# A chunked mLSTM cell feeding a squared-ReLU FFN: chunks 4 and 5 moved to the quarter-array layout, and the first FFN2 placed ahead of the third FFN1

## The chip, the core and the metric

The kernel runs on one core of one Trainium2 chip. The metric is the device time of one execution in microseconds (us), lower is better. All counting below starts at 0: chunk `s` is tokens `128 s` to `128 s + 127`, group `g` is chunks `2g` and `2g + 1`. (The change's own words count from 1: its "chunks 5 and 6" are `s = 4, 5`, its "first" and "third group" are `g = 0, 2`.)

## What is computed

An mLSTM cell (4 batches, 8 heads, 768 tokens, head size 40) and then a feed-forward layer on its 3072 rows of 320 numbers. The reference, cut to its core:

```python
for t in range(S):
    m_new = np.maximum(f_gate[:, :, t] + m, i_gate[:, :, t])
    f_stab = np.exp(f_gate[:, :, t] + m - m_new)
    i_stab = np.exp(i_gate[:, :, t] - m_new)
    m = m_new
    C = f_stab[..] * C + i_stab[..] * np.einsum('bhd,bhe->bhde', vt, kt)
    n = f_stab[..] * n + i_stab[..] * kt
    h_tilde = np.einsum('bhde,bhe->bhd', C, qt)
    denom = np.maximum(np.abs(np.einsum('bhd,bhd->bh', n, qt)), 1.0)
    y[:, :, t] = sigmoid(o_gate[:, :, t]) * h_tilde / denom
x = y.transpose(0, 2, 1, 3).reshape(B * S, H * D)     # 3072 x 320
h = np.maximum(x @ w_in, 0.0)                         # w_in 320 x 2048
out = h * h @ w_out                                   # w_out 2048 x 320
```

## The kernel before

The recurrence is done in chunks of 128 tokens: 24 chunks, 6 per batch. For a chunk, `scores` (L554) multiplies keys by queries, `weigh` (L494) makes the decay weights with ScalarE from a broadcast gate row block `A` (loaded by `load_A`, L425, masked by `mask`, L465, on GpSimd), `weighted` (L587) multiplies both on VectorE, and an attend step multiplies the result by the values, adds what comes from the state `C` of the chunk before, and makes the next state. The rows then become `x`, and `x` is turned so that its columns lie on partitions (`xT`). FFN1 of a group of two chunks needs both `xT`; FFN2 needs the squared result `g2`.

There are two forms of this attend step.

- **Full array, chunks 0 to 5** (`X_SQ = 6`): `attend` (L609) uses 128x128 matmuls: `hi` (state times queries, L622), `dC` (new state, L634) and `hp` (weights times values, L645). VectorE joins and normalises them (`normalise`, L805), and `turn_rows` (L843) turns `x` with four matmuls and a ScalarE copy (L853).
- **Quarters, chunks 6 to 23**: `attend_begin` (L684) and `attend_end` (L743) use 64x64 quarters of the array (L708 state times queries, L727 weights times values, L738 new state). Between the two stands a one-element VectorE instruction, L700: it reads what the first half wrote, and the second half's L738 waits for it. The result is transposed by VectorE in 32x32 squares (L758) and then goes out to HBM and back: `store_num` (L772), `load_num` (L775), `normalise_turned` (L783) on VectorE, `store_rows` (L826), `load_rows` (L830), and a VectorE square transpose `turn_squares` (L838). All these transfers are issued by SyncE, whose queue is served in the order written: a transfer that waits holds up those behind it. This form needs the decayed queries `eA` (`decays`, L480, ScalarE; `scale_q`, L669, VectorE) and its state in another layout (`decay_C`, L674).

FFN1 of groups 0 and 1 is the plain product, four parts each (`ffn1`, L890). From group 2 on it is a seven-product scheme (`ffn1_open` L1058, `ffn1_rows` L1078, `ffn1_close` L1095) on sums of weights (`sums_of_win`, L1014: `WS[0]`, `WS[1]`, `WS[3]`, and F21 in place) and of x (`sums_of_x`, L1028). FFN2 of group 0 is plain (`ffn2`, L906); from group 1 on it is a seven-product scheme as well (`ffn2_fast`, L970), on sums of `w_out` (`sums_of_weights`, L935: T0, T1, T2, and in place) and of `g2` (`sums`, L948: S1, S2, A21 in place, S4). These sums are VectorE work.

The weights arrive as 64-bit words and are rounded to 32 bits in 18 pieces (10 of `w_in`, 8 of `w_out`): a SyncE `fetch` (L195), two ScalarE passes `words` (L212), three VectorE passes and one on GpSimd in `join` (L225).

The order on every engine is written out by hand (`manual_schedule`); there is no planner. The program has three stretches:

1. a start-up until chunk 2 (L1153 to L1223),
2. the loop `u = 0..7` (L1228 to L1293) with chunks 2 to 5: even `u` does scores and weights, odd `u` attends, and each `u` carries one part of FFN1 of group 0 or 1,
3. the loop over `parts` (L1317 to L1430): part `n` belongs to chunk `s = 6 + n // 4`, at step `at = n % 4`. Before the change the parts are FFN1 of group 2 (n = 0..3), FFN2 of group 0 (4..7), FFN2 of group 1 (8..11), FFN1 of group 3 (12..15), and so on.

## Time and profile before

| what | us |
|---|---|
| three runs: median, lowest, highest | 492.46, 490.75, 492.82 |
| the profiled execution, its own time | 491.22 |
| its span, first to last instruction | 489.4 |
| TensorE matmul (PE) busy in the span | 481.7 |
| TensorE weight loads (PEld) | 449.0 |
| VectorE (DVE) | 341.8 |
| ScalarE (ACT) | 240.4 |
| GpSimd (POOL) | 215.3 |
| granted TensorE clock | 0.999 |

The profile names an instruction by engine, source line, and the tiles that it writes and reads. A float32 matmul leaves two records and its weight load two, so a count of "x16" is eight matmuls. The chain of waits is the sequence of work that ended last, followed backwards from the end; the list of waits says which engine stood idle for which other. Times in a timeline are counted from the start of the span.

### The profile page before, as it was taken

The numbers are of one execution on the slowest core, as the hardware profiler recorded it, in microseconds if no ns is written. First come the engines' busy times: TensorE is split into PE (matmuls) and PEld (weight loads), VectorE is DVE, ScalarE is ACT, GpSimd is POOL, SyncE is SP. The second block draws the span as 40 slices with busy tenths as digits, with TensorE's granted clock in tenths as the row PEclk, the third lists the DMA queues.
The fourth block names the chain that finished last, engine by engine and source line by source line (L and its number), as shares of the span: only waits on it lengthen the run. The fifth ranks groups of instructions, "written<-read, shape, count | busy, mean of one in ns | idle before, by whom it ended". The sixth has DMA issues, their size and how long they took to land.

```text
span 489.4 us, 15237 instructions
## 1 busy us (share of the span) xinstructions
PE 481.7 (98%) x6169; PEld 449.0 (92%) x6169; DVE 341.8 (70%) x704; ACT 240.4 (49%) x531; POOL 215.3 (44%) x322
## 2 busy tenths in 40 slices
PE   9999999999999999999999999999999999999997
PEld 4886788897799999999999999999999999999996
DVE  7799767888946856957966956857856956635441
ACT  4676996764522650942742941742942640513300
POOL 6455533432679178078179078078174040020000
PEclk9999999999999999999999999999999999999999
DMA  9999997745878579758759778658665612200000
GB/s 185 227 243 227 304 230 183 151 84 140 171 130 199 120 138 225 134 107 212 135 99 219 140 117 208 134 109 213 123 106 129 149 51 82 55 28 2 3 27 29
DMA packets 191096, 68.08 MB, mean 139 GB/s; under 512 B 158833, under 2 KB 180241, under 8 KB 191025
## 3 DMA queue, kind: packets, MB, share of 16 engines
q1 hardware_dynamic: 185280, 57.50, 55.1%
q0 software_dynamic: 5600, 9.50, 8.1%
q8 instruction: 49, 0.80, 0.7%
q14 instruction: 23, 0.18, 0.1%
q10 hardware_dynamic: 144, 0.10, 0.1%
HBM read 54.77 MB, written 18.01 MB: 149 GB/s over the span
## 4 chain that ended last, share of the span: by engine, by line
PE 87%; ACT 5%; SPq 4%; DMA 3%; issue 1%; DVE 0%; ACTq 0%
PE h_ps L965 35%; PE h_ps L1041 26%; PE h_ps L1090 8%; PE h_ps L911 4%; PE h_ps L874 3%; PE numT L727 3%; PE numT L708 2%; DMA lent_t<-in_moe_w_in_dram 1%; PE numT L738 1%; SPq L210 1%; PE tp L575 1%; PE h_ps L575 1%; SPq L1151 1%; ACT g_c L511 1%; DMA raw<-in_moe_w_in_dram 1%; DMA og<-in_o_gate_dram 1%
## 5 line engine op out<-in xcount | busy, mean ns | idle before, releaser
L475 POOL TENSOR_SCALAR_AFFINE_SELECT A_bc<-A_bc 64x512 f32<-64x512 f32 x32 | 22.5, 704 | 80.4 <-ACT kq L492 57.9
L965 PE MATMUL h_ps<-T,S 128*128 128x160 f32 x352 | 51.7, 300 | 0.6 <-ACT g_c L1107 0.6
L1071 ACT COPY r_sb<-h_ps 128x512 f32<-128x512 f32 x18 | 10.5, 585 | 84.2 <-PE h_ps L1041 84.2
L965 PEld LDWEIGHTS h_ps<-T,S 128*128 128x128 f32 x352 | 48.9, 190 | 1.1 <-ACT g_c L1107 0.9
L965 PE MATMUL h_ps<-w_out,g 128*128 128x160 f32 x336 | 49.2, 303 | 0.0
L981 DVE TENSOR_TENSOR y_sb<-y_sb,h_ps 128x160 f32<-128x160 f32 x44 | 14.1, 320 | 47.7 <-PE h_ps L965 47.6
L965 PEld LDWEIGHTS h_ps<-w_out,g 128*128 128x128 f32 x336 | 46.1, 190 | 1.3 <-issue 0.5
L1041 PE MATMUL h_ps<-xT,w_in 128*128 128x128 f32 x320 | 42.8, 278 | 0.0
L1041 PE MATMUL h_ps<-lent_t,w_in 128*128 128x128 f32 x320 | 42.2, 275 | 0.0
L1041 PEld LDWEIGHTS h_ps<-xT,w_in 128*128 128x128 f32 x320 | 38.9, 192 | 1.4 <-issue 1.0
L1090 PE MATMUL h_ps<-xT,w_in 64*64 64x128 f32 x960 | 39.1, 272 | 0.0
L1041 PEld LDWEIGHTS h_ps<-lent_t,w_in 128*128 128x128 f32 x320 | 38.9, 192 | 0.2 <-issue 0.2
L1041 PE MATMUL h_ps<-lent_t 128*128 128x128 f32 x320 | 39.0, 275 | 0.0
L1041 PEld LDWEIGHTS h_ps<-lent_t 128*128 128x128 f32 x320 | 37.3, 192 | 0.0
L505 ACT ACTIVATE A_bc<-A_bc,b_R 128x64 f32<-128x64 f32 (+1 forms) x128 | 35.7, 361 | 1.8 <-POOL A_bc L475 1.4
L1090 PEld LDWEIGHTS h_ps<-xT,w_in 64*64 64x64 f32 x960 | 34.8, 133 | 1.3
L379 POOL DMA_DIRECT2D va<-in_v_dram x56 | 34.2, 619 | 1.8 <-DMA kq_rows<-in_q_dram 1.3
L758 DVE STREAM_TRANSPOSE tn<-numT 128x256 f32<-128x256 f32 x36 | 14.0, 428 | 28.5 <-PE numT L708 19.2
L874 PE MATMUL h_ps<-xT,w_in 128*128 128x256 f32 x128 | 30.1, 385 | 1.6 <-ACT xT L853 1.2
L874 PEld LDWEIGHTS h_ps<-xT,w_in 128*128 128x128 f32 x128 | 23.4, 190 | 6.1 <-POOL w_in L240 1.6
L1033 POOL TENSOR_TENSOR lent_t<-xT 128x128 f32<-128x128 f32 (+1 forms) x18 | 14.6, 833 | 32.7 <-DVE xT L840 32.7
L965 PE MATMUL h_ps<-w_out,g_c 128*128 128x160 f32 x192 | 28.0, 302 | 0.0
(218 smaller groups left out, 1150.0 us busy)
## 6 DMA issues: line engine op xcount, KB each, us to landing
A_bc<-a_slots SPq DMA_DIRECT2D x32, 256.0 KB, 4.4
num_rows<-tn SPq DMA_DIRECT2D x18, 256.0 KB, 2.3
kq<-num_rows SPq DMA_DIRECT2D x72, 64.0 KB, 2.1
raw<-in_moe_w_out_dram SPq DMA_DIRECT2D x7, 640.0 KB, 5.4
kqT<-kq_rows SPq DMA_DIRECT2D x34, 128.0 KB, 3.3
og<-in_o_gate_dram SPq DMA_DIRECT2D x24, 160.0 KB, 4.9
out_dram<-y_sb SPq DMA_DIRECT2D x24, 160.0 KB, 3.1
raw<-in_moe_w_in_dram SPq DMA_DIRECT2D x7, 512.0 KB, 6.9
```

The costliest lines, as they stand in the source:

```text
L379: eng.dma_start(dst[HALVES[n], PR * (1 - late_keys) : PR * (2 - late_keys)], src[HALVES[late_keys], PR * m : PR * (m + 1)],)
L475: nc.gpsimd.affine_select(part, part, compare_op=ALU.is_ge, fill=-1e30, base=0, pattern=[[0, PR], [0, 2], [1, DP]], channel_multiplier=-1,)
L505: nc.scalar.activation(A[0][:, x, to], A[0][:, x, to], AF.Exp, bias=b_R[:, b, c, own, x : x + 1],)
L727: nc.tensor.matmul(d["numT"][m][HALVES[e], i, t0:], lhsT=va_w[s % NKQ][keys, at * D1 : at * D1 + DP], rhs=rhs, start=(s % NB == 0 and i == ...
L758: nc.vector.transpose(to[:, 2 * m : 2 * m + 2], d["numT"][m].rearrange("p c t -> p (c t)"))
L874: nc.tensor.matmul(hs[i][:, n, :], lhsT=w_in[:, a, fb * P : (fb + 1) * P], rhs=xT[:, :, a, :], start=(n == 0 and a == 0), stop=False,)
L911: nc.tensor.matmul(o_ps, lhsT=st["g2", g][:, fb, j * P : (j + 1) * P], rhs=w_out[:, fb, :], start=(fb == 0), stop=(fb == NF - 1),)
L965: nc.tensor.matmul(to, lhsT=lhsT[:, p], rhs=rhs[:, p, :], start=(start and p == 0), stop=(p == NPAIR - 1), skip_group_check=True,)
L981: add = lambda to, a, b: nc.vector.tensor_tensor(to, a, b, op=ALU.add)
L1033: sub = lambda to, a, b: eng.tensor_tensor(to, a, b, op=ALU.subtract)
L1041: nc.tensor.matmul(to[:, n, :], lhsT=lhsT[:, 4 * q + n, :], rhs=rhs, start=(start and n == 0), stop=True, skip_group_check=True,)
L1090: nc.tensor.matmul(to[cols, n, :], lhsT=w_in2[rows, 4 * q + n, cols], rhs=rhs, start=(start and n == 0), stop=True, skip_group_check=True,)
```

## The change

- `X_SQ` goes from 6 to 4: chunks 4 and 5 use `attend_begin` and `attend_end`, and their `x` goes the HBM way. They keep their scores on full width, and their state stays in the older buffers (`C_flat`), of which chunk 4 reads the full layout and chunk 5 the quarter layout.
- In loop `u`: chunk 4's weights and decays are made at `u = 2` ahead of a rounding step, from the unmasked `A`, and masked afterwards (`mask_W`). `decays` and `scale_q` for chunks 4 and 5 are added, `turn_rows` of 4 and 5 is gone. `store_num`, `load_num`, `normalise_turned`, `store_rows`, `load_rows`, `turn_squares` of 4 and 5 are spread from `u = 5` to `n = 2`.
- FFN2 of group 0 becomes `n = 0..3` and FFN1 of group 2 `n = 4..7`. The four matmuls on the last two pieces of `w_out` rows come at the end of FFN2 (`F2`), with two PSUM banks open.
- FFN1 of group 2 no longer begins its first product ahead (`ffn1_begin` is gone).
- Loads of k and v of chunks 8 and 9 go from the SyncE queue (`u = 5, 7`) to the GpSimd queue (`n = 2, 3`); o gates of 8 to 11 come at `n = 3, 4`.
- `sums_of_win(3)` and `(2)` move to `n = 3`, `sums_of_weights` to `n = 3` (T0) and `n = 4` (T1, T2), `sums(1, ..)` S1 and S2 to `n = 6, 7`.
- Chunk 0's state is copied in its two diagonal halves in place of a product with a block mask.

The core of the diff:

```diff
-    KQ_SQ, X_SQ, ROT = 7, 6, 8
+    KQ_SQ, X_SQ, ROT = 7, 4, 8
...
-    def ffn2(g, j, part):
+    F2 = [(j, fb) for half in ((0, 8), (8, 14), (14, 16)) for j in range(GT) for fb in range(*half)]
+
+    def ffn2(step):
+        if step == 0:
+            st["o_ps"] = [ps_h.tile([P, W], F32, name="h_ps")[:, :DM] for _ in range(GT)]
+        for j, fb in F2[8 * step : 8 * step + 8]:
...
             if u == 2:
+                weigh(4, masked=True, vw=False)
+                decays(4)
                 rounding.words()
             weighted(s)
...
             if u == 2:
-                mask(s + 1)
                 rounding.join()
+                mask_W(4)
                 rounding.join()
-                weigh(s + 1, masked=True)
+                values(4)
                 rounding.words()
             else:
                 if u == 0:
                     relu_half()
-                weigh(s + 1, masked=(u == 0), vw=(u > 0))
+                weigh(s + 1, masked=(u != 6), vw=(u == 6))
+                if u == 4:
+                    mask_W(5)
                 square_half()
+                if u > 0:
+                    scale_q(s)
...
-            attend(s)
+            if s < X_SQ:
+                attend(s)
+            else:
+                attend_begin(s)
+                attend_end(s)
+                store_num(s)
...
-                rounding.join()
+                rounding.join(fetch=u < 7)
...
-            for r in {5: (8,), 7: (9,)}.get(u, ()):
-                load(r)
-            for r in {5: (7,), 7: (8,)}.get(u, ()):
-                pair_up(r)
+            if u == 5:
+                pair_up(7)
+            if u == 7:
+                load_A(7)
             if u > 4:
-                load_o(2 * s)
-                load_o(2 * s + 1)
+                load_num(s)
             transposes(s + 1, (True, True))
             rounding.words()
             ffn1(u // 4, u % 4)
             square_half()
+            if u == 5:
+                decays(5)
+            if u == 7:
+                normalise_turned(4)
+                store_rows(4)
+                rounding.fetch()
+                rounding.join()
...
+        if u == 6:
+            load_squares(7)
...
-    turn_rows(5)
-    load_squares(7)
...
-    parts = [(1, 2, i) for i in range(4)] + [(2, 0, i) for i in range(4)]
-    for g in range(1, NG):
+    parts = []
+    for g in range(NG):
         parts += [(2, g, i) for i in range(4)]
         if g + 2 < NG:
             parts += [(1, g + 2, i) for i in range(4)]
-    LAST = (17, 17, 17, 17, 18)
+    ROUNDED = (16, 18)
...
+        if n == 0:
+            turn_kq(7)
+            pair_up(8)
+            load_rows(4)
+            normalise_turned(5)
+            store_rows(5)
+            rounding.words()
...
+            if n == 1:
+                turn_squares(4)
+                load_rows(5)
             do(store_num, s)
-            do(load_num, s)
-            do(load_squares, s + 2)
+            if n == 1:
+                load_squares(8)
+                load_num(6)
+            else:
+                do(load_num, s)
+                do(load_squares, s + 2)
...
+        if n == 2:
+            weigh(7, masked=True)
+        if n == 3:
+            normalise_turned(6)
+            store_rows(6)
+            load_o(8)
+            load_o(9)
+            load_rows(6)
+            sums_of_win(3)
+            sums_of_win(2)
+        if n == 4:
+            sums_of_weights(1)
...
+            if n == 2:
+                turn_squares(5)
+                sums_of_x(2)
+            else:
+                do(normalise_turned, s)
+                do(store_rows, s)
...
+        if n in (2, 3):
+            load(6 + n)
+        if n == 4:
+            load_o(10)
+            load_o(11)
...
+        for x in {3: (0,), 4: (2,)}.get(n, ()):
+            sums_of_weights(x)
+        if n in (6, 7):
+            sums(1, slice(0, NPAIR), (n - 5,))
```

The new `mask_W` sets the weights of later tokens to zero in place of the `-1e30` that `mask` writes into `A`:

```python
def mask_W(s):
    nc.gpsimd.affine_select(
        st[s]["W"], st[s]["W"], compare_op=ALU.is_ge, fill=0.0, base=0, pattern=[[0, H], [1, P]],
        channel_multiplier=-1,
    )
```

## What the change should do: the prediction

> **What bounds the kernel now.** I read the page first: busy time by engine, then the shares of the chain.
>
> ```profile
> PE 481.7 (98%) x6169; PEld 449.0 (92%) x6169; DVE 341.8 (70%) x704; ACT 240.4 (49%) x531; POOL 215.3 (44%) x322
> ...
> PE 87%; ACT 5%; SPq 4%; DMA 3%; issue 1%; DVE 0%; ACTq 0%
> ```
>
> TensorE is the chain for 87% of the span. The chain in order of time says where: until 60.56 us it runs through ScalarE, transfers and their issue, from there to the end almost only through TensorE. So in the stretch that the change rewrites (59 to 130 us) a matmul removed is time gained, unless TensorE then waits. The list of TensorE's waits shows how few there are:
>
> ```profile
> PE h_ps L874 <- ACT xT L853: 1.2, 1, 1.2
> ...
> PE numT L738 <- DVE kq L700: 0.3, 1, 0.3
> ```
>
> The 1.2 us ends at 60.56, ahead of FFN1 at `u = 4`. The chain's rows price both forms of attend (start, us, what):
>
> ```profile
> 65.35 1.05 PE hi L622 x8
> 66.40 0.89 PE dC L634 x8
> 67.29 1.75 PE hp L645 x16
> ...
> 114.54 0.38 PE numT L708 x8
> 114.92 0.44 PE numT L727 x16
> 115.36 0.26 PE numT L738 x16
> 115.61 0.02 issue
> 115.64 0.17 DVE kq L700
> 115.80 0.04 issue
> 115.85 0.44 PE numT L738 x16
> 116.29 0.46 PE numT L727 x16
> 116.75 0.22 PE numT L708 x8
> 116.97 13.12 PE h_ps L911 x48
> ```
>
> Full array: 3.69 us for chunk 4. Quarters: 2.43 us for chunk 7, the stop for L700 included.
>
> VectorE is the next engine. In the stretches (PE, PEld, DVE, ACT, POOL busy) it is 82 and 89% busy while TensorE hardly waits:
>
> ```profile
> 91.06:110.04 18.98, 18.98 (x338) 18.39 (x337) 15.50 (x35) 12.60 (x26) 6.72 (x10) 1.00 0.58 103
> 110.04:130.09 20.05, 19.77 (x148) 13.86 (x152) 17.91 (x32) 10.82 (x26) 9.10 (x13) 1.00 0.62 145
> ```
>
> [...] a quarter matmul record L727 lasts 0.27 us, yet 16 take 0.44. [...] `num_rows<-tn` lands after a median 2.3 us, and SyncE waits for such a store 18 times, at most 4.0. [...]
>
> **The change part by part.** PE terms, from the chain:
>
> 1. Chunk 4's attend: 3.69 to 2.43, gain 1.26.
> 2. Chunk 5's attend: `hi` 1.05 and `hp` 1.75, 2.80 together; as quarters without a new state 0.38 + 0.44 + 0.46 + 0.22 and a stop of 0.25 to 0.3, 1.8. Gain 1.0.
> 3. Two `turn_rows`: 0.37 + 0.37 each, gain 1.47. Their ScalarE copies go too.
> 4. FFN1 of group 2: 6.50 + 1.77 + 6.45 + 1.91 = 16.63 before; the later groups' form, which it takes, is 3.57 + 1.77 + 9.13 + 1.91 = 16.38. Gain 0.25. FFN2 of group 0 keeps 32 matmuls (17.6). In chunk 7 FFN1's rows now stand between the halves and cover L700: gain 0.3.
> 5. The 1.2 us wait. ScalarE stood idle 4.27 us before the words at 48.93 (a raw piece was late), and ran without a pause to the copy that TensorE waited for. Chunk 4's weights (2.43 + 0.20) move from behind those words into that idle time, with `decays` (1.25): 3.9 us. `A` of chunk 4 was issued at 35.33, issued in 0.76, and landed 8.9 later: 45.0; 45.0 + 3.9 = 48.9, just in time. The copy then follows the relu of FFN1 part 3 (PE ends 57.5, relu 1.0, copy 0.5): about 59.1, and scores end at 59.3. Gain 1.1; if `A` is late, each us takes one from it, so 0 to 1.2.
>
> Sum of gains: 1.26 + 1.0 + 1.47 + 0.55 + 1.1 = 5.4.
>
> What is added beside TensorE. GpSimd: two `mask_W`, not in the trace; the nearest row is `mask` (1.09 to 1.28), which they replace, in gaps of 1.6 and more. Bound: 0 to 0.5; I take 0, it cannot gain. Chunk 5's `decays` (1.25) meets 1.55 of ScalarE idle. k and v of chunks 8, 9: 14 issues, 2 x 4.5 us on GpSimd's queue; behind them stands `mask` of chunk 8 at `n = 5`, some 8 us later, so 0. SyncE loses these and gains the round trips.
>
> The last pieces of `w_out`: after chunk 6's attend, VectorE does transposes, copies, a square transpose and the first join by 3.4 us, GpSimd adds 1.55: 5.0. First use is the fifth matmul of `n = 2`, at 4.4 + 2.2 = 6.6. Covered.
>
> **Where TensorE may now wait: L700 of chunk 7 (`n = 5`).** VectorE works in order, from chunk 6's attend to that L700 (steps from start to start in its timeline): transposes, copies 1.07; square transpose 0.46; two joins 3.8; `scale_q` 0.61; `weighted` 1.2; square transpose 0.46; `sums_of_x` 1.06 (8.7 so far); `normalise_turned` 1.84; two win sums 2.3; T0 to T2 4.26; U2 and U4 1.3. Together 18.4. TensorE reaches L738's second half after 3 x 4.4 (FFN2) + 3.57 + 1.1 + 1.77 = 19.6. So VectorE has 1.2 to spare, and `normalise_turned(6)` waits for a load that is behind five others on SyncE. From VectorE's transposes of chunk 5: store_num to next issue 2.0, load_num 2.3, store_rows(4) 0.4; its landing (109.66 to 113.24 in the trace) 3.6; load_rows(4) 1.9, store_rows(5) and landing 3.6, load_rows(5) 1.9, store_num(6) 0.35, load_squares(8) 2.5, load_num(6) 2.3, landing 2.1: 22.9. TensorE passes from there to the end of chunk 6's attend in 12.4, so the rows land at 10.5, when VectorE has been free since 8.7. It idles 1.8 and with small gaps 2.1; less the 1.2: a stall of 0.9.
>
> **And L700 of chunk 8 (`n = 9`).** In the same place two parts later in the trace before, VectorE starts FFN1's four adds at 167.33, does `turn_kq`, `weighted`, S3 and the y add, and L700 at 173.33; TensorE needs it at 173.95, 0.6 later. After the change S2 (1.2) and T3 (1.4) stand in this row too, and S1 ahead of it fills the 0.5 that VectorE waited at 202.55. 2.6 - 0.6 = 2.0 at most; as the adds can start some 0.5 before 167.33's place, 1.5. From `n = 10` on the order is as before.
>
> Net: 5.4 - 0.9 - 1.5 = 3.0 gained. Against the profiled execution's own 491.22 (span 489.4 and 1.8 around it): 488.2. That execution lies 1.2 below the median 492.46; the four known times average 491.8, so I forecast 491.8 - 3.0 = 488.8. About 0.5% (2.5 us) is what a measurement of this kernel can tell from no change.
>
> **Rivals.**
>
> - *No new stall.* If transfers land faster than their medians and VectorE's steps keep their covers: 491.8 - 5.4 = 486.4. For: DMA share falls to 0.58 in this stretch, and the SyncE queue loses 14 issues. Against: 18.4 of 19.6 leaves little.
> - *VectorE becomes the bound from `n = 1` to 9.* The sums of `w_in`, `w_out` and `g2`, which lay in FFN2 of group 0, now lie around FFN1's adds. If the two stalls double to 4.8: 491.8 - 0.6 = 491.2, between 490 and 493. For: 89% busy before. Against: the load is mostly the same work in another order.
> - *The SyncE round trips are late: slower.* One mechanism: the five stores and loads ahead of load_num(6) are each released by the landing before. At the longest waits in the trace before (4.0 for num_rows, 4.7 for x_rows, 6.2 for a load of xT) N of chunk 6 lands 8 to 9 us later, VectorE stands, and L700 of chunk 7 with it, us for us: 488.8 + 8 = 497. It decides for slower by over 0.5% from 5.5 us of lateness. For: DMA share was 0.9 at 60 to 91 us. Against: the later chunks' same transfers kept near the medians, and a one-hop delay is not five.
>
> **Numbers.** Forecast 0.46 (487.2 to 490.3), no stall 0.14, VectorE-bound 0.22, late round trips 0.18. Range 485.8 to 493.2: it holds the first three. Faster: nearly all of the forecast and no stall, 0.59. Same: the VectorE case and a rest, 0.24. Slower 0.17.
>
> **What would show it.** Right: L622 and L645 only for chunks 0 to 3; the FFN1 part of `u = 4` starts near 59.4; the `n = 8` scores near 127 in place of 130.09; new waits of PE for L700 or for U2, U4 near 111 and 131, 2 to 3 us in sum; a VectorE wait for `num_rows` of chunk 6. Wrong: a wait of TensorE over 3 us after 60 us, SyncE waiting over 4 us for `x_rows` near 90, or `n = 8` later than 130.

## The result: slower by 0.8%

| | us |
|---|---|
| before, six runs: median, lowest, highest | 492.32, 490.75, 492.9 |
| after, six runs: median, lowest, highest | 495.77, 494.76, 496.75 |
| after / before, 95% interval | 1.0077 [1.0055, 1.0099] |
| profiled execution after: own time, span | 496.75, 495.0 |

The forecast was 488.8, its range ended at 493.2. Medians here and below are over all executions of a kernel, while the ratios leave out those more than 1.5% above its quickest (three of e14's 22, one of e8's six). The two profiled executions lie 5.5 us apart, more than the medians (3.45), since the profiled one of before is a quick one and that of after the slowest of its six. All accounts below are between the two executions.

TensorE's own work did become less. The page of the changed kernel (busy us by engine; then shares of the chain):

```profile
PE 479.6 (97%) x6227; PEld 447.1 (90%) x6229; DVE 341.8 (69%) x719; ACT 242.7 (49%) x534; POOL 226.6 (46%) x335
...
PE 64%; DMA 10%; DVE 8%; POOL 5%; SPq 5%; ACT 4%; issue 3%; DVEq 0%; POOLq 0%; ACTq 0%
```

That is 2.1 us less of TensorE than before, but TensorE's share of the chain fell from 87 to 64%: in some places other engines and transfers now end last. TensorE's waits of after (us in total, times, longest):

```profile
PE h_ps L1089 <- DVE r_sb L1072: 3.2, 1, 3.2
PE numT L757 <- DVE kq L718: 1.8, 4, 0.8
...
PE h_ps L1056 <- issue: 0.8, 1, 0.8
PE h_ps L896 <- ACT xT L875: 0.8, 1, 0.8
PE numT L727 <- issue: 0.7, 1, 0.7
PE h_ps L980 <- DVE S L975: 0.7, 1, 0.7
```

Before, the list held 1.2, 0.3 and (at 353.00) 0.6 from 60 us on. (Lines of after: L718 is the stop, the one-element instruction between the halves, that was L700; L727, L746, L757 are the quarters that were L708, L727, L738. U2 and U4, L1072 and L1074, are VectorE's sums of FFN1's first products, and FFN1's rows, L1089, need U2. S1 and S2 are sums of `g2`, T0 to T3 sums of `w_out`; FFN2 at n = 8 needs S2.) The windows of after from the scores of chunk 6 on (n = 0 to 3, 4 to 7, 8 to 11; columns: length, busy PE, PEld, DVE, ACT, POOL, granted clock, DMA share, GB/s):

```profile
86.22:108.23 22.01, 21.16 (x179) 15.24 (x176) 17.59 (x37) 8.93 (x18) 12.85 (x17) 1.00 0.69 156
108.23:131.75 23.52, 20.36 (x321) 19.70 (x323) 19.79 (x40) 11.07 (x27) 12.78 (x19) 0.93 0.90 164
131.75:152.47 20.72, 19.27 (x265) 18.43 (x257) 15.82 (x28) 10.52 (x26) 14.72 (x23) 1.00 0.72 128
```

Where the time went, by start times of the same work in both:

| place | before | after | after is later by |
|---|---|---|---|
| scores of chunk 6 (n = 0) | 89.97 | 86.22 | -3.75 |
| n = 8 | 130.09 | 131.75 | 1.66 |
| last half of attend, chunk 8 (n = 9) | 137.0 | 140.6 | 3.6 |
| the same, chunk 10 | 173.8 | 179.0 | 5.2 |
| the same, chunk 22 | 393.8 | 399.8 | 6.0 |

So 3.75 us were gained and 5.41 lost again by n = 8: TensorE waited 4.0 us where it had waited 0.3 (22.01 - 21.16 and 23.52 - 20.36), and its busy time grew by 1.7. The granted clock of 0.93 in the 23.52 us accounts for the latter: 3.4 us at half clock (116.60 to 120.01) cost 1.7. In windows of 4 us one sees where: behind the 3.17 us wait.

```profile
113.00:117.00 4.00, 0.83 (x18) 0.63 (x20) 3.86 (x4) 0.00 (x0) 3.91 (x5) 0.95 1.42 164
117.00:121.00 4.00, 4.00 (x95) 3.83 (x88) 1.72 (x4) 0.00 (x0) 0.00 (x0) 0.62 0.67 167
121.00:125.00 4.00, 4.00 (x37) 4.00 (x38) 3.10 (x8) 0.90 (x2) 0.46 (x1) 1.00 0.65 148
```

(A DMA share above 1 means that packets which start in the window last beyond it.)

Why was U2 late? VectorE's timeline of after shows two stops and then a full row ahead of it (start, us; in brackets idle time and what ended it):

```profile
99.66 1.71 DVE L231 TENSOR_SCALAR mag<-mag 128x640 int32<-128x640 int32 x1
...
104.96 1.29 DVE L601 TENSOR_TENSOR A_bc<-h_ps,A_bc 128x512 f32<-128x512 f32 x2 [2.13 <-POOL vw L536]
...
108.25 0.17 DVE L812 TENSOR_SCALAR dm<-kq 128x8 f32<-128x8 f32 x1 [0.34 <-DMA kq<-num_rows]
...
110.11 1.22 DVE L1041 TENSOR_TENSOR lent_t<-w_in,lent_t 128x1024 f32<-128x1024 f32 x1
111.24 1.22 DVE L1039 TENSOR_TENSOR w_in<-w_in 128x1024 f32<-128x1024 f32 x1
112.38 1.48 DVE L954 TENSOR_TENSOR T<-w_out 128x1280 f32<-128x1280 f32 x1
113.89 1.83 DVE L956 TENSOR_TENSOR T<-w_out,T 128x1280 f32<-128x1280 f32 x1
115.64 0.68 DVE L1072 TENSOR_TENSOR r_sb<-h_ps,r_sb 128x512 f32<-128x512 f32 x1
```

`weighted(7)` (L601) waited 2.13 for `values(7)` (L536 on GpSimd), which stands behind the last two joins. Those follow VectorE's passes over the last two pieces of `w_out` (97.39 to 102.23), which stand behind chunk 6's transposes and chunk 4's square transpose, and of which one, L231, took 1.71 in place of 0.49. The chain of waits of after shows the start and the end of this row:

```profile
87.93 6.17 DMA raw<-in_moe_w_out_dram
94.11 0.02 issue
94.12 2.68 DMA xT<-x_rows
...
102.38 1.84 POOL w_out L236
104.22 0.70 POOL vw L536
```

`normalise_turned(6)` (L812) then still had to wait 0.34 for its rows. So there are two sources, one behind the other, and the sums stand behind both: from 108.25 on VectorE worked without a pause until U2.

### The profile page after: what moved, and what is told of

Same layout as the page of the kernel before. It is cut to its first block, busy times and chain, and to the rows that moved or that the text cites. A ratio compares the mean times of both kernels' runs of the same rounds, so it can differ in the third digit from the quotient of the medians.

```text
span 495.0 us, 15400 instructions
## 1 busy us (share of the span) xinstructions
PE 479.6 (97%) x6227; PEld 447.1 (90%) x6229; DVE 341.8 (69%) x719; ACT 242.7 (49%) x534; POOL 226.6 (46%) x335
## 4 chain that ended last, share of the span: by engine, by line
PE 64%; DMA 10%; DVE 8%; POOL 5%; SPq 5%; ACT 4%; issue 3%; DVEq 0%; POOLq 0%; ACTq 0%
PE h_ps L980 29%; PE h_ps L1056 19%; PE h_ps L1089 6%; DMA raw<-in_moe_w_out_dram 3%; PE numT L746 2%; PE h_ps L896 2%; PE numT L727 2%; POOL va L375 2%; DMA lent_t<-in_moe_w_in_dram 1%; PE numT L757 1%; SPq L1149 1%; DMA x_rows<-x_sb 1%; DVE mag L231 1%; SPq L206 1%; DMA num_rows<-tn 1%
## 5 line engine op out<-in xcount | busy, mean ns | idle before, releaser
L478 POOL TENSOR_SCALAR_AFFINE_SELECT A_bc<-A_bc 64x512 f32<-64x512 f32 x32 | 24.9, 779 | 84.1 <-ACT kq L496 49.7
L1070 ACT COPY r_sb<-h_ps 128x512 f32<-128x512 f32 x20 | 11.7, 586 | 86.3 <-PE h_ps L1056 86.3
L1089 PE MATMUL h_ps<-xT,w_in 64*64 64x128 f32 x960 | 41.1, 278 | 3.2 <-DVE r_sb L1072 3.2
L1089 PEld LDWEIGHTS h_ps<-xT,w_in 64*64 64x64 f32 x960 | 36.3, 136 | 4.7 <-DVE r_sb L1072 3.4
L375 POOL DMA_DIRECT2D va<-in_v_dram x64 | 39.4, 627 | 1.6 <-PE numT L727 1.1
```

Of the source, the lines that this page charges most:

```text
L375: eng.dma_start(dst[HALVES[n], PR * (1 - late_keys) : PR * (2 - late_keys)], src[HALVES[late_keys], PR * m : PR * (m + 1)],)
L478: nc.gpsimd.affine_select(part, part, compare_op=ALU.is_ge, fill=-1e30, base=0, pattern=[[0, PR], [0, 2], [1, DP]], channel_multiplier=-1,)
L1070: nc.scalar.copy(m1[:], X[:])
L1089: nc.tensor.matmul(to[cols, n, :], lhsT=w_in2[rows, 4 * q + n, cols], rhs=rhs, start=(start and n == 0), stop=True, skip_group_check=True,)
```

## The experiments

All are timed against the kernel before on the same chip. Where nothing else is said, the edit is to the changed kernel. "Stop of chunk 8" is the last half of its attend (before 137.0, after 140.6).

### One part alone: the order (e8, e8b) and the early weights (e11)

```diff
-    KQ_SQ, X_SQ, ROT = 7, 4, 8
+    KQ_SQ, X_SQ, ROT = 7, 6, 8
...
-            load_rows(4)
-            normalise_turned(5)
-            store_rows(5)
```

(and `turn_rows` of 4 and 5 back, their decays, stores, loads and `turn_squares` away.)

> One part of the change alone: FFN2 of group 0 ahead of FFN1 of group 2 and all that is moved with it, but chunks 4 and 5 on the full array with turn_rows (X_SQ = 6), so without their round trips. If the order alone makes the loss: TensorE's work is 3.7 us more than in the changed kernel, U2 waits 2 to 3 us and S2 up to 3, time 495 to 499. If the round trips of chunks 4 and 5 on SyncE are what makes chunk 6 and 7 late: no wait over 1 us after 86 us, time 491 to 493.

e8 took 506.86 us. It loads chunk 7's squares at u = 6 into the buffer that chunk 5's product still reads, so chunk 5 is computed from other queries, and TensorE waited 6.2 us for that load. So it tells nothing of the order; e8b has the load behind the loop.

> One part of the change alone, e8 without its mistake (there the squares of chunk 7 were loaded into the buffer that chunk 5 on the full array still reads; now the load comes behind the loop, as before the change): FFN2 of group 0 ahead of FFN1 of group 2, chunks 4 and 5 on the full array with turn_rows. If the order alone makes the stalls (values(7) behind the joins, N of chunks 6 and 7 late): U2 and S2 wait 2 to 5 us together, time 493.5 to 497. If the round trips of chunks 4 and 5 make them: no wait over 1 us after 86 us, time 491 to 492.5.

496.70 us, 1.0090 [1.0063, 1.0117]. With no round trip of chunks 4 and 5 at all, the waits are there: U2 1.42, the product at n = 8 2.17, the stops 0.41 and 1.30, in sum 5.3; VectorE stood 2.12 for `values(7)` and 1.47 for the rows of chunk 7. The granted clock of this execution was 1.00, so the waits alone make its loss. The order, with the early weights in it, costs about 4.4 us. The whole change has 495.77: of the 3.7 us that the quarters take from TensorE about 1 arrives by the medians, and as the intervals overlap, it may be none.

e11 is the kernel before with step 5 alone:

```diff
             if u == 2:
+                weigh(4, masked=True, vw=False)
                 rounding.words()
...
-                mask(s + 1)
                 rounding.join()
+                mask_W(4)
                 rounding.join()
-                weigh(s + 1, masked=True)
+                values(4)
```

> One part alone, in the kernel before: chunk 4's weights ahead of the rounding words at u = 2, masked afterwards (mask_W). The prediction's step 5: TensorE's wait of 1.2 us at 60.56 goes, gain 1.1. The theory from the trace of after: the words then wait for the next raw piece instead, FFN1 at u = 4 starts at the same time, within 0.3 us, and the time does not change (ratio within 0.998 to 1.002).

491.55 us over 22 runs, 0.9984 [0.9972, 0.9996]: 0.8 us gained (0.2 to 1.4). The ratio lies within the 0.998 to 1.002 that I expected for no change, but its interval leaves no change out; the prediction's 1.1 is within it. In its profiled execution the wait was still there (1.17), as in after (0.84). Among the other traces below with the early weights, e1, e3, e9, e14, e15 and e16 have no such wait and the rest 0.9 to 1.2: it goes in some executions and not in others. In after, ScalarE made the weights in its gap, and then waited 2.48 us for the next raw piece:

```profile
44.63 2.46 ACT L515 ACTIVATE g_c<-A_bc,b_T 128x128 f32<-128x128 f32 x8
...
52.41 0.81 ACT L216 ACTIVATE mag<-raw 128x640 f32<-128x640 f32 x1 [2.48 <-DMA raw<-in_moe_w_out_dram]
```

### The first wait, U2 (e1 to e4)

e1 puts `values(7)` ahead of the joins on GpSimd:

```diff
-        if n == 2:
-            weigh(7, masked=True)
...
+        if n == 1:
+            rounding.words()
+            weigh(7, masked=True)
         if n < len(ROUNDED):
             while rounding.done < ROUNDED[n]:
```

> One step moved: GpSimd makes values(7) ahead of the last two joins, not behind them. Theory A (two waits in a row on VectorE: weighted(7) for values(7), 2.13 us, then normalise_turned(6) for its rows, which land near 107.9 whatever weighted does): weighted(7) starts about 2 us earlier (near 102.8), normalise_turned(6) only about 0.3 earlier, U2 near 115.3, and the time stays within 0.5 us of the changed kernel (495 to 496). Theory B (the wait for values(7) alone makes U2 late): U2 near 113.6, PE's wait falls from 3.2 to about 1.1, time about 493.

e2 is e1 and on SyncE:

```diff
+                load_num(6)
                 load_squares(8)
-                load_num(6)
```

> As e1, and load_num(6) is issued ahead of load_squares(8) on SyncE. Theory A: both waits of VectorE shrink, the rows of chunk 6 land about 1 us earlier (near 106.9), U2 about 1.3 earlier (near 114.3), PE's wait about 1.9 in place of 3.2, time about 494. Theory B: the same as e1, since the order on SyncE does not matter. The rival of the prediction (late round trips on SyncE set the end): gain of 2 us or more over e1.

e3:

```diff
-        if n == 4:
-            sums_of_weights(1)
...
-        for x in {3: (0,), 4: (2,)}.get(n, ()):
+        for x in {3: (0,), 5: (1,), 7: (2,)}.get(n, ()):
```

> Only T1 and T2 are moved: T1 from ahead of U2 to the end of n = 5, T2 from behind U4 to the end of n = 7. The theory that VectorE's row holds up TensorE: U2 1.8 earlier (near 113.8), PE's wait at L1089 about 1.4, the stop L718 of chunk 7 some 3.3 earlier; of these up to 3.3 us can come back as waits at n = 8 and 9 (S2, L718 of chunk 8). Time 493 to 495.5. If VectorE's content over n = 0 to 9 is what bounds, and not its order, the time stays at 495.8, with the stall at n = 7 to 9 instead.

e4 is e1, and `normalise_turned(6)` with its store and load goes from n = 3 to the end of n = 4, behind U2 and U4:

```diff
         if n == 3:
-            normalise_turned(6)
-            store_rows(6)
...
-            load_rows(6)
...
         if n == 4:
+            normalise_turned(6)
+            store_rows(6)
+            load_rows(6)
             load_o(10)
```

> As e1, and normalise_turned(6) with its store and load goes behind U2 and U4, so that nothing ahead of U2 waits for the rows of chunk 6. Theory A: VectorE goes on without the second wait, T1 ends near 111.8, U2 near 112, PE's wait falls to 0.5 or less, the granted clock in n = 4 to 7 goes back near 1.00 if its drop came from the wait, and the time falls by 3 to 4.5 us, to 491.5 to 493. If VectorE's content bounds: the wait only moves to L718 of chunk 7 or to n = 8, time 494.5 to 496.

| | U2's wait | wait for S2 | half clock behind | median | ratio |
|---|---|---|---|---|---|
| after | 3.17 | 0.66 | 3.4 | 495.77 | 1.0077 |
| e1 | 1.15 | 3.38 | 3.0 | 496.66 | 1.0101 |
| e2 | 0.79 | 6.88 | 5.8 | 500.66 | 1.0178 |
| e3 | 1.18 | 5.08 | 4.8 | 498.92 | 1.0141 |
| e4 | none | 4.59 | 6.2 | 498.61 | 1.0134 |

("Half clock behind" is how many us TensorE ran at a granted clock of 0.50 after the longest wait; in after these 3.4 us cost 1.7.) Each edit shortened U2's wait, and none made the kernel faster. What was taken from U2 came back, with more, at S2 (L975, n = 8), four parts later. In e1 VectorE and SyncE show why; first VectorE, then SyncE's queue:

```profile
124.24 0.68 DVE L687 TENSOR_TENSOR kq<-kq,kqT 128x512 f32<-128x512 f32 x1
127.49 0.24 DVE L812 TENSOR_SCALAR dm<-kq 128x8 f32<-128x8 f32 x1 [2.56 <-DMA kq<-num_rows]
...
130.54 0.68 DVE L1106 TENSOR_TENSOR r_sb<-r_sb,h_ps 128x512 f32<-128x512 f32 x1
...
132.92 1.22 DVE L975 TENSOR_TENSOR S<-S,g 128x1024 f32<-128x1024 f32 x1
```

```profile
112.47 1.89 SPq L855 DMA_DIRECT2D xT<-x_rows  x4
114.52 0.84 SPq L942 DMA_DIRECT2D out_dram<-y_sb  x2
115.40 1.79 SPq L343 DMA_DIRECT2D kq_rows<-in_k_dram  x2
117.24 1.23 SPq L343 DMA_DIRECT2D kq_rows<-in_q_dram  x2
118.52 1.21 SPq L413 DMA_DIRECT2D og<-in_o_gate_dram  x2
119.82 0.74 SPq L795 DMA_DIRECT2D num_rows<-tn  x1
122.90 1.76 SPq L800 DMA_DIRECT2D kq<-num_rows  x4
```

The rows of chunk 7 were asked for at 122.90 and were there at 127.49; FFN1's last adds and S2 stand behind them on VectorE. Their store, issued at 119.82, had stood behind issues of k, q and o gates on SyncE since 117.7, when VectorE had the result, and their load went out 2.3 us after that issue had ended (120.56). In after the rows are there in time, as TensorE came to chunk 7 some 3 us later. Of e1's two theories neither holds whole. U2's wait fell to the 1.15 of theory B (1.1), because the rows of chunk 6 landed earlier too (11.1 us after the attend in place of 12.8; the reason isn't shown), while theory A had them fixed. The time went as A had it, but for another reason: with U2 repaired, the next round trip through HBM is the bound.

### The second wait, S2 and FFN1's adds (e5, e6, e7, e12)

e5 computes S1 and S2 at n = 6 ahead of `normalise_turned(7)`, in place of n = 6 and 7 behind it:

```diff
+            if n == 6:
+                sums(1, slice(0, NPAIR), (1, 2))
...
                 do(normalise_turned, s)
```

> The changed kernel with S1 and S2 of group 1 at n = 6 ahead of normalise_turned(7), not behind it. The theory now: there are two choke points, U2 at n = 4 and S2 at n = 8; S2 is late because normalise_turned(7), ahead of it on VectorE, waits for the rows of chunk 7, whose round trip through HBM runs on SyncE's clock and not on TensorE's. In the changed kernel U2's 3.2 us wait hides most of that. So here U2's wait stays at about 3, TensorE's waits for S2 (0.66) and for L718 of chunk 8 (0.79) go, and the time falls by 1 to 1.5, to about 494.5. If VectorE's content bounds n = 8 to 11 and not that wait, L718 of chunk 8 stays late and the time stays at 495.8.

497.79 us, 1.0102 [1.0065, 1.0138]. U2 waited 2.97 as expected, the wait for S2 went, the stop of chunk 8 waited 1.54. The time did not fall, so the expectation was missed; the interval contains the 1.0077 of after, so this is no gain, but not a shown loss either.

e6 is e1 and, on SyncE, `store_num(7)` ahead of `pair_up(9)` and of `load_o` of 10 and 11:

```diff
             do(store_num, s)
+            if n == 5:
+                pair_up(9)
```

> As e1, and on SyncE store_num(7) is issued ahead of pair_up(9) (which then fills the time until load_num(7) may go) and of load_o of chunks 10 and 11. Theory (round trip of chunk 7 makes S2 late): the rows of chunk 7 land 1 to 2 us earlier than in e1 (there 127.4), TensorE's wait for S2 falls from 3.4 to between 1.2 and 2.4, the clock stays near 1.00, time 1.5 to 3 us below e1's 496.7, so 493.5 to 495. If VectorE's content makes S2 late: no change from e1.

495.73 us, 1.0058 [1.0032, 1.0084]; the profiled execution had U2 1.26, S2 0.66, stop of chunk 8 0.79, clock 0.999. The rows of chunk 7 landed 7.5 us after the attend, in e1 10.5, and the wait for S2 fell from 3.38 to 0.66, further than the 1.2 to 2.4 expected, so the round trip of chunk 7 was its cause. The time is 0.9 below e1, less than the 1.5 to 3 expected, and the intervals overlap.

e7 has e1, e4 and e6's order on SyncE, and S1, S2 and T2 ahead of `normalise_turned(7)`:

```diff
+            if n == 6:
+                sums(1, slice(0, NPAIR), (1, 2))
+                sums_of_weights(2)
...
                 do(normalise_turned, s)
...
-        for x in {3: (0,), 4: (2,)}.get(n, ()):
+        for x in {3: (0,)}.get(n, ()):
...
-        if n in (6, 7):
-            sums(1, slice(0, NPAIR), (n - 5,))
```

> All together: values(7) ahead of the joins, normalise_turned(6) behind U2 and U4, S1, S2 and T2 of n = 6 ahead of normalise_turned(7), store_num(7) ahead of pair_up(9) and load_o. Theory: neither U2 nor S2 waits longer than 0.5 us, no clock drop, n = 8 starts near 127, and what is left are about 1 us at n = 0 to 3 and 1 us from n = 12 on: 488.5 to 491, below both kernels. If the content of VectorE bounds n = 1 to 9: another wait of 2 us or more at L718 of chunk 7 or 8, time 492 to 495.

495.93 us, 1.0060 [1.0039, 1.0082]. TensorE no longer waits for U2, but for FFN1's adds at n = 7 (1.75) and at the stop of chunk 8 (1.34). The first of the two expected cases is out. The second, VectorE's row, is nearer, but its wait at the stop was to be 2 us or more. e12 moves `normalise_turned(7)` of e7 behind those adds:

```diff
+                if n == 7:
+                    normalise_turned(7)
+                    store_rows(7)
+                    load_rows(7)
...
-            else:
+            elif n != 6:
                 do(normalise_turned, s)
```

> e7 with normalise_turned(7), its store and its load behind FFN1's last four adds of n = 7, so that no PSUM bank of FFN1 is held up by the round trip of chunk 7. If that round trip is what held TensorE at n = 8 in e7 (1.75 us for the adds): that wait goes, n = 8 starts near 127.5; L718 of chunk 8 stays late by about 1 us, since VectorE now does the normalising between the adds and it; time 493 to 494.5 against e7's 495.9. If not: 495.5 or more.

497.05 us, 1.0095 [1.0067, 1.0124]. The adds' wait went, but waits for `weighted(8)` (2.04) and at the stop (1.50) took its place, so the expected gain was missed.

### What holds VectorE: leave work or waits out (e9, e13, e14)

e9 is e7 without the four subtractions of T0 to T3, so FFN2 from group 1 on multiplies by other weights:

```diff
-            nc.vector.tensor_tensor(T[0], B12, B11, op=ALU.subtract)
...
-            nc.vector.tensor_tensor(B12, B22, B12, op=ALU.subtract)
+        T.update({0: B12, 1: B22, 2: B21})
```

> e7 with the sums T0 to T3 left out (the products take the plain quarters of w_out in their place, so FFN2 of groups 1 and up computes something else): 5.9 us less work for VectorE in n = 3 to 8, nothing changed on the other engines. If VectorE's content over n = 1 to 9 is what holds TensorE once the order is mended: the waits at U2, S2, the adds of n = 7 and L718 of chunk 8 fall to under 1 us in sum, time 489 to 491.5. If queues and round trips hold it: the same waits as e7, time 494.5 to 496.

495.92 us, 1.0054 [1.0030, 1.0077], the same as e7. In the trace the stop of chunk 8 came at 137.1, 1.7 earlier than in e7, and VectorE used part of its free time to wait: 1.38 for the rows of chunk 7, 0.52 for the squares of chunk 9. The trace of e7 is its slowest execution, so the lead of 1.5 us that e9 has at the end is none in the medians. TensorE's waits named in the expectation (here for the adds and at the stop) sum to 1.5 (e7: 3.1), between its two cases.

e13 is e1 with the rows of chunk 5 in place of those of 6 and 7:

```diff
+        if s in (6, 7):
+            st[s]["N"] = kq_b[0][:, 1].rearrange("p h d -> p (h d)")
```

> e1 with normalise_turned of chunks 6 and 7 reading the rows that came back for chunk 5 (already in its buffer), so that neither waits for its own round trip; the loads of both chunks are still issued, into a buffer that nothing reads. The output rows of chunks 6 and 7 are thereby other ones; all work stays. If the round trips of chunks 6 and 7 are what makes U2 and S2 late: VectorE's waits for num_rows near 105 and 125 go, TensorE's wait at U2 falls from 1.1 to about 0.5, its wait for S2 from 3.4 to under 1, the clock stays near 1.00, time 491 to 493 against e1's 496.7. If not (content of VectorE, GpSimd): 495 or more.

494.74 us, 1.0065 [1.0037, 1.0094], 1.9 below e1. U2's wait fell to 0.23 and S2's to 0.65, clock 1.00, stop of chunk 8 at 137.2. VectorE now worked from 102.65 to 137.00 with two stops of 1.23 and 0.91 for TensorE and none for a transfer, and the stop still came 0.95 late. The 491 to 493 expected was missed, and the interval overlaps that of e1, so the 1.9 us are not clear of noise. What the traces show is that without the round trips the two waits and the half clock go: the round trips were a cause, worth about 2 us by the medians, and behind them stands VectorE's own row.

e14 takes away both, on e1:

```diff
+        if s in (6, 7):
+            st[s]["N"] = kq_b[0][:, 1].rearrange("p h d -> p (h d)")
...
-            nc.vector.tensor_tensor(T[0], B12, B11, op=ALU.subtract)
...
+        T.update({0: B12, 1: B22, 2: B21})
```

> e13 (no wait for the round trips of chunks 6 and 7) and besides the sums T0 to T3 left out, as in e9. Theory: two rows of about equal length hold TensorE over n = 1 to 9, VectorE's content and the round trips, so that taking away one alone (e9, e13) shows little. Then both together give 3 us or more: no wait over 0.6 us from 86 us until n = 9, the stop of chunk 8 near 134 (before: 137.0, e9: 137.1, e13: 137.2), time 490.5 to 492.5. If a third thing holds it (GpSimd's values, the squares of chunk 9): chunk 8 near 136 or later, time 494 or more.

493.50 us over 22 runs, 1.0019 [0.9999, 1.0039]: 3.2 below e1 by the medians, 4.0 by the ratios, and clear of its interval. So the two together hold most of what the new order costs. That each holds a like part is likely (1.9 for the first by e13, the rest for the second), but neither step is clear of noise by itself. The median is 1 us above the expected range, and the profiled execution shows a third cause, the one that the expectation named for that case:

```profile
130.16 1.22 DVE L967 TENSOR_TENSOR S<-S,g 128x1024 f32<-128x1024 f32 x1
134.08 1.25 DVE L405 STREAM_TRANSPOSE kqT<-kqT 128x1024 f32<-128x1024 f32 x1 [2.70 <-DMA kqT<-kq_rows]
```

The squares of chunk 9 are again behind chunk 7's store and load on SyncE (issued 127.48). And FFN2 waited 1.66 for a late piece of `w_out`, as VectorE stood 2.47 for chunk 4's rows (L864, until 98.07) ahead of the joins: a round trip of a chunk that the change moved, which this edit leaves in.

### GpSimd and the supply of instructions (e10, e15)

e10 is e7 with T0 to T2 on GpSimd at n = 4, 5 and 6:

```diff
-            nc.vector.tensor_tensor(T[0], B12, B11, op=ALU.subtract)
+            nc.gpsimd.tensor_tensor(T[0], B12, B11, op=ALU.subtract)
...
-        for x in {3: (0,)}.get(n, ()):
+        for x in {4: (0,), 5: (1,), 6: (2,)}.get(n, ()):
```

> e7 with T0, T1 and T2 computed on GpSimd at n = 4, 5 and 6. VectorE has 4.5 us less in n = 3 to 6, GpSimd some 9 more. If VectorE's content is the bound and GpSimd has the room (it is busy for half of this stretch): 490 to 492.5, at or below the kernel before. If GpSimd's mask and values come late behind the sums, or VectorE's instructions stretch beside them: 494 or more.

499.10 us, 1.0146 [1.0111, 1.0180]. It is the second case: S1 on VectorE, 1.22 us elsewhere, took 5.55 and ended 1.1 after T2 on GpSimd, and TensorE waited 4.5 us for FFN1's adds. VectorE, then GpSimd:

```profile
124.78 5.55 DVE L975 TENSOR_TENSOR S<-g 128x1024 f32<-128x1024 f32 x1
```

```profile
126.32 2.92 POOL L958 TENSOR_TENSOR T<-w_out,T 128x1280 f32<-128x1280 f32 x1
```

e15 puts 46 tiny products in place of 6 idle ones at the start:

```diff
-    idle(12)
+    idle(6)
+    t = ps_h.tile([P, W], F32, name="idle", tag="h_ps")
+    for _ in range(46):
+        nc.tensor.matmul(t[:, :16], lhsT=zeros[:, :1].to_broadcast([P, P]), rhs=zeros[:, :16], start=True, stop=True)
```

> The changed kernel with 46 tiny products in place of 6 idle ones in TensorE's start-up, so 40 more instructions ahead of everything. For the waits of TensorE that the profile puts down to nothing (issue: 87.60, 160.84, 344.58 in the changed kernel). If they come from the supply of TensorE's instructions, they move to 40 matmuls earlier in the program (out of the attend of chunk 19, for one); if they belong to those places (a semaphore that the profile doesn't show), they stay there. The time stays within 1 us of the changed kernel's.

496.74 us, as after. Of the three waits that the profile puts down to "issue", the one at n = 0 stayed (0.32), those at 160.84 (0.85) and 344.58 (0.74) were gone, and one of 0.27 came at 233.90. The one near 344 is in all twelve other traces of the new order with both chunks in quarters, so it seems to hang on the count of TensorE's instructions and not on its place; the one near 160 is missing in e2, e3, e9 and e12 too, so a single trace doesn't tell. That it is the supply of instructions is my estimate and is not shown.

### The quarters without the order (e16, e17)

The kernel before, early weights, and chunk 4 alone in quarters (e16; its new state is written in chunk 5's full layout, `turn_rows(4)` is gone, and chunk 0's state is copied in halves as in the change):

```diff
+            if s == 4:
+                attend_begin(s)
+                attend_end(s)
+                store_num(s)
...
+                if u == 6:
+                    normalise_turned(4)
+                    store_rows(4)
```

> The kernel before, with chunk 4's weights early as in e11, and chunk 4 alone in quarters: its rows have the time from u = 5 to n = 0 for their round trip, so the order of FFN1 and FFN2 and every engine's order from n = 0 on stay as before the change; chunk 5 stays on the full array. TensorE's work shrinks by 1.26 (attend) and 0.74 (turn_rows), 2.0 us. If the quarters pay wherever the round trip has room, and the loss of the change is its order: scores of chunk 6 start 1.5 to 2 us earlier than before (89.97), no new wait over 0.5 us, time 489.5 to 491, below both kernels and e11's 491.55. If the quarters cost as much as they save (round trip late, VectorE late): 492 or more.

496.32 us, 1.0089 [1.0060, 1.0117], so the 489.5 to 491 was missed. `normalise_turned(4)` lies where VectorE stood 3.87 us for its rows, ahead of other work. e17 moves it behind the rounding step and the win sum of u = 6:

```diff
-                if u == 6:
-                    normalise_turned(4)
-                    store_rows(4)
...
+        if u == 6:
+            normalise_turned(4)
+            store_rows(4)
```

> e16 with normalise_turned(4) and store_rows(4) moved from ahead of u = 6's rounding step to behind it and behind the win sum. In e16 VectorE stood 3.87 us for the rows of chunk 4 (they came at 78.4) with the rounding steps, the win sum and chunk 5's normalise queued behind, and turn_rows(5) waited 3.3 us and FFN1 1.3 us for that. Here those steps fill the wait: VectorE reaches normalise_turned(4) near 77.5 and waits about 1. TensorE then has its 2.0 us of work less and the 0.9 us of the wait at 60.56 that e16 showed gone: time 489.5 to 491, below both kernels, if the loss of the change lies in its order. If 493 or more: the round trip of chunk 4 costs what the quarters save even here.

497.36 us, 1.0105 [1.0073, 1.0138], missed as well. The round trip doesn't fit where I took it to have room. VectorE's view of e17:

```profile
80.35 0.90 DVE L818 TENSOR_SCALAR dm<-kq 128x8 f32<-128x8 f32 x1 [1.25 <-DMA kq<-num_rows]
...
93.98 0.58 DVE L868 STREAM_TRANSPOSE xT<-xT 128x384 f32<-128x384 f32 x1 [2.81 <-DMA xT<-x_rows]
```

From `store_num(4)` at 69.28 to the square transpose of the rows at 93.98 are 24.7 us; TensorE had 20.9 us between (69.28 to 90.20, to the end of the products before FFN1), waited 4.46 at FFN1 and then ran at a clock of 0.82 for 16 us. So by this trace the quarters need some 25 us of other work behind them at this place of the program (an estimate from one execution). The order of before has not so much; the new order has it, but puts FFN1's adds among the waits.

## Why the prediction was wrong, by its own steps

It forecast a gain of 3.0 us. The medians show a loss of 3.45, the two profiled executions one of 5.5.

- **Steps 1 to 3 (3.73 us less for TensorE by n = 0): right.** Chunk 4's attend took 65.21 to 67.64, 2.43; chunk 5's 78.79 to 80.77, 1.98, where 1.8 was expected; the scores of chunk 6 came 3.75 earlier.
- **Step 4 (0.25 of form, 0.3 of cover): wrong.** From n = 0 to n = 8 TensorE was busy for 39.84 us before and 41.52 after; without the 1.7 of the half clock that is 39.8, so the 0.25 didn't show. The cover only changed place: before, FFN1's rows stood between chunk 6's halves, and after, chunk 6 has the open stop, with 0.52 in place of the 0.28 of chunk 7. First before, then after:

```profile
97.97 0.39 PE L738 MATMUL numT<-vw,kq 64*64 64x41 f32 x16
98.18 1.17 PE L1090 MATMUL h_ps<-xT,w_in 64*64 64x128 f32 x33
...
99.95 0.39 PE L738 MATMUL numT<-vw,kq 64*64 64x41 f32 x16
```

```profile
92.56 0.39 PE L757 MATMUL numT<-vw,kq 64*64 64x41 f32 x16
92.77 1.08 PE L579 MATMUL h_ps<-kqT 40*64 40x128 f32 x32
94.37 0.44 PE L757 MATMUL numT<-vw,kq 64*64 64x41 f32 x16 [0.52 <-DVE kq L718]
```

- **Step 5 (1.1, bounds 0 to 1.2): too high for the profiled pair, fair for the median.** The trace of after has 0.06 (60.50 for 60.56), e11 0.8. "Just in time" held for `A`; the step left out that another raw piece was late two instructions further on.
- **The stall at the stop of chunk 7 (0.9): this step failed, and with it the sign.** Its sum put VectorE's row at 18.4 us against a deadline of 19.6 for the last entry. Measured: 3.17 at U2, and a lower clock behind it. The sum had two faults. First, U2, inside the row, has a deadline of its own: FFN1's rows need it, at 113.2 in the trace, 17.9 us after VectorE began on chunk 6's attend at 95.3. Without U4 and T2 the prediction's own terms make 16.3 up to U2 and 18.4 with its 2.1 of idle time, so this alone would have been a stall of 0.5. Second, the way to U2 took 21.0 (95.33 to 116.32). VectorE idled 2.97 (0.50 for chunk 4's rows, 2.13 for `values(7)`, 0.34 for chunk 6's rows), and L231 and T1 took 1.6 longer than elsewhere. The rows of chunk 6 came at 12.9 where 10.5 was expected, and the 2.13 us for GpSimd ahead of them was missed, because moved instructions were followed on VectorE and not on the engine that feeds them. The two waits overlap: without the one for GpSimd VectorE would have stood for the rows in its place, had these come when they did.
- **The price of a stall: missing.** Each us of stall was counted as one us. The 3.17 us were followed by a granted clock of 0.50 from 116.60 to 120.01, 1.7 us more of TensorE's time. Over the traces the clock fell to 0.50 for 3.4 us or a multiple of it in 16 of the 20 (left aside the end of the span, where before has it as well, from 488.1 on), and with each of the eleven waits of 2.9 us or more there was such a fall, in the wait or up to 1.5 us behind it. Of the shorter waits some had it as well: two of 2.04 and 1.50 in e12, and single ones of 1.54 in e5 and 1.17 in e11, while 2.17 in e8b and 2.39 in e10 brought none. So in these traces a short wait sometimes had this price; what decides it they don't show. The wait of e11 ended at 61.25:

```profile
61.30:64.70 3.40, 3.40 (x8) 2.77 (x9) 1.89 (x4) 3.29 (x10) 1.37 (x2) 0.50 1.27 150
```

The other executions show it as well: of the twelve of e9 the four with a mean clock of 1.000 took 493.1 to 495.0 us, the other eight 495.4 to 497.0; of the six of after the only one at 1.000 is the fastest, 494.76. That is still 2.4 above before's median, so the clock is a part of the loss and not the whole.

- **The stop of chunk 8 (1.5): right in size.** S2 0.66 and L718 0.79, 1.45.
- **"From n = 10 on the order is as before" (0): wrong.** From the stop of chunk 8 to that of chunk 22 2.4 us more were lost. Each wait made what followed later by a little more than its own length: the two "issue" waits by 1.0 each, the small ones (0.20, 0.25) by 1.0 together, and the 0.64 at 353.00 that only before has takes 0.7 off. The time of e15 did not fall with its two "issue" waits, because the waits at S2 and at the stop of chunk 8 were 1.2 and 1.3 there, 1.0 more than in after, and 5.5 us at half clock followed U2's wait in place of 3.4.
- **A slip in the signs.** "n = 8 near 127" does not follow from the sums: 5.4 less 0.9, all of it ahead of n = 8, gives 125.6. It came at 131.75.
- **The rivals.** "VectorE becomes the bound from n = 1 to 9" (0.22) came near in size: its stalls of 4.8 were 5.1 (0.52, 3.17, 0.66, 0.79). As a mechanism it is one of two causes (e13, e14). It gave 491.2 because it had neither the clock nor what followed. "SyncE's round trips are late" named the right chain with the wrong chunk: N of chunk 6, its rows read back, was 2.4 late, not 8, but as soon as U2 was repaired, N of chunk 7 on the same queue held S2 (e1 to e4), and e13 puts both at about 2 us by the medians. A stall with two or more causes in parallel is not a sum of rivals of which one is right.

What stays open: the intervals of the kernels e1, e5, e7, e9, e12 and e15 overlap, so small gains among them are not told apart; how the loss of the order splits between VectorE's row and the round trips is not measured clear of noise; and in e6, e9 and after the rows of chunk 11 came 1.4 to 3.7 us later against TensorE's place than before, for which I have no cause (in e11, which is faster, they came 1.2 later too). Of all kernels here only e11 is faster than before, by 0.16%.

## What to carry to other kernels

Work that was taken from the busiest engine counted here only as far as everything else that feeds it came earlier too (3.75 us gained by the scores of chunk 6, 5.41 lost again by n = 8): before you move a product whose PSUM banks VectorE must empty into a stretch, list for each of these evictions its own deadline and all that stands ahead of it, with the waits of the engines that feed it. In the chain of transfers (store, load, store, load) a wait that was removed at one place came back at the next: in e1 U2's fell from 3.17 to 1.15 and S2's rose from 0.66 to 3.38. And TensorE's stall of 3.17 us cost 1.7 us more than its length.

## What the runs showed that was not expected

- Three of VectorE's steps took longer beside GpSimd's work. In after, L231 at 99.66 took 1.71 in place of 0.49 while a join ran on GpSimd from 99.30 to 101.02, and L823 at 91.42 took 1.96 in place of 0.29 beside `mask(7)` (92.12 to 93.22); they ended 0.2 to 0.4 us after GpSimd's step. In e10 S1 took 5.55 for 1.22, from 124.78 on; GpSimd was issuing transfers from 124.25 to 126.32 and then did T2, which ended 1.1 before S1. Why they took longer is not shown. With T0 to T2 on GpSimd e10 took 499.10 us, where e7 took 495.93.
- A quarter chunk's way from `store_num` to turned rows took 24.7 us in the busy stretch from 69 us on (e17), of which VectorE's share was under 4.
- TensorE had waits that nothing in the profile releases (0.3 to 0.9 us in after, up to 2.4 in e10). Two of them, at 160.84 (0.85) and 344.58 (0.74) in after, were gone with 40 more instructions ahead (e15).
